# Products with the values in two row tiles of 64 keys, the last 8 keys of all heads in one block, and v loaded over all partitions

## The chip, the core and the metric

The kernel runs on one core of a Trainium2 chip. TensorE (PE; its weight loads are listed as PEld), VectorE (DVE), ScalarE (ACT), GpSimd (POOL) and the DMA queues, of which SyncE (SP) issues most, work side by side and meet at semaphores. The metric is the device time of one execution in microseconds; the time of a kernel is the median of its runs.

## What is computed

An attention over pooled keys and values, then a layer ("mixture of depths") in which only 128 of the 576 rows of each batch go through a dense network. All data is fp32.

```python
B, H, S, D = 8, 8, 576, 64;  pool = 8;  Sp = S // pool          # 72 pooled keys
k_p = k.reshape(B, H, Sp, pool, D).mean(axis=3)
v_p = v.reshape(B, H, Sp, pool, D).mean(axis=3)
scores = scale * np.matmul(q, k_p.transpose(0, 1, 3, 2))
attn = softmax(scores)                                           # over the 72 keys
x = np.matmul(attn, v_p) -> (B, S, H * D)
...
scores = np.einsum('bsd,d->bs', x, w_gate)                       # one gate value per row
for b in range(B):
    top_idx = np.argpartition(-scores[b], capacity)[:capacity]   # the 128 largest
    h = np.maximum(x[b, top_idx] @ w1, 0.0)                      # 512 -> 1024
    out[b, top_idx] += sigmoid(scores[b, top_idx])[:, None] * (h @ w2)
```

## The kernel before

**Order.** `direct_path` first registers about 970 small operations with a planner (`add`: engine, a cost, a function, the buffers that it reads and writes). A list of numbers written out by hand, `ORDER`, then gives the order in which they are issued. Each engine takes its own operations in that order; a number is the position in which the operation was registered. The costs play no part when the kernel runs. Waits follow from the buffers.

**Stages of one batch.** `load_k`, `load_q`, `load_v` are DMAs on SP. `pool_k` and `k_trans` (DVE) add up and transpose the keys into KT; `q_trans` (DVE, L452) transposes q into QT. `scores` (PE, L467) computes the transposed scores, keys on partitions, in 32x32 tiles of the array, 24 matmuls for one parity `s` of the heads and one part `h` of the rows (256 or 320 columns); `CELLS` says which 32 keys of which heads land where. ACT takes the exp into ET (L478). The eight heads' 72 keys make 576 key rows for each of the 8 x 576 query rows, and each parity has four heads, so 288 key rows: three blocks `t`, in which pairs of heads (`PAIRS`) share the 128 partitions, 64 + 64 or 96 + 32 keys at a time.

`pool_v` adds the 8 rows of each value window: on POOL in three steps (L499, L503, L507), in batch 0 and for one block of batch 1 on TensorE with a unit matrix (L494, `sums`), whose result ACT copies out (`copies`, L516). The result is VS, one tile for each block, with two more columns: the constant 8 for the softmax sum, and the product with the gate's weights (`gates`: L522 and the DVE sum L526). `spread` (ACT, L530, seven copies per batch by `PIECES`) then puts the pieces of VS into VP, a tile that is zero elsewhere: each head of a pair has its own columns, so one matmul over 128 keys can serve two heads.

`attend` (L537) forms the product for a chunk of 128 rows (four chunks) or 64 rows (the fifth): for each block and parity one fp32 matmul, ET as the weights, 132 columns of VP moving, accumulated over the three blocks in one PSUM bank for each parity (pA, or pX for some chunks of the first two batches). In the profile an fp32 matmul is two weight loads and two matmuls. `zs` (ACT, L572 and L573) reads the sums and the gate values, `norm` (DVE, L579 and L583) divides, and the rows are stored. `rank` finds the 128 largest rows, a gather brings them back, and `dense` runs them through w1 (`up`, L695) and w2 (`down`, L705) with the whole 128x128 array; its matmuls stand between other batches' work in `ORDER`.

**Opening.** 28 matmuls of zeros (L299) go ahead of the first work of TensorE. ACT fills parts of VR with zeros (L311, four fillings) because some partitions of a block receive no load. `weights` (L339) writes the constant 8 into VS.

**Loads of v.** `RUNS` (L395) has seven DMAs a batch: one of 512 KB and two of 256 KB, over 64 partitions each, and four of 32 KB.

Of the kernel before, what the change touches and what calls it, by code (L numbers as in the profile page):

```python
# [16 lines left out]
def kernel(  # L17
# [34 lines left out]
    54, 53, 1, 35, 56, 0, 4, 2, 38, 57, 5, 37, 32, 6, 33, 36, 34, 51, 7, 8, 39, 9, 10, 50, 52, 11, 12, 40, 62,  # L52
    13, 14, 60, 64, 15, 16, 17, 63, 18, 66, 19, 55, 20, 21, 67, 61, 22, 42, 98, 59, 65, 58, 97, 23, 24, 48, 25,
    46, 78, 26, 49, 77, 27, 68, 44, 28, 45, 81, 29, 43, 30, 47, 31, 41, 106, 96, 70, 74, 88, 71, 105, 85, 72,
    76, 84, 79, 69, 87, 107, 73, 89, 86, 75, 80, 164, 92, 113, 165, 108, 114, 119, 115, 109, 170, 90, 116, 162,
    93, 94, 120, 95, 163, 117, 101, 110, 169, 121, 186, 111, 257, 166, 112, 123, 258, 118, 122, 173, 255, 91,
    193, 256, 103, 124, 174, 104, 83, 187, 102, 252, 180, 194, 179, 195, 99, 254, 125, 196, 188, 126, 189, 100,
    197, 82, 245, 171, 3, 132, 247, 253, 172, 168, 167, 128, 200, 181, 133, 246, 248, 175, 129, 134, 305, 198,
    130, 140, 176, 298, 190, 131, 136, 141, 249, 358, 299, 366, 177, 142, 137, 306, 135, 191, 251, 143, 199,
    250, 201, 192, 138, 127, 178, 300, 307, 285, 362, 313, 182, 202, 144, 203, 145, 204, 360, 286, 146, 206,  # L60
    368, 147, 308, 292, 205, 148, 301, 207, 149, 183, 150, 139, 365, 151, 184, 208, 479, 152, 259, 478, 211,
    153, 185, 154, 361, 287, 155, 209, 156, 288, 309, 210, 215, 157, 312, 291, 158, 359, 212, 310, 367, 289,
    213, 260, 216, 363, 314, 302, 217, 219, 303, 290, 315, 214, 316, 293, 475, 311, 411, 223, 304, 317, 220,
    318, 221, 294, 319, 364, 224, 412, 261, 225, 413, 320, 414, 295, 227, 369, 296, 218, 321, 159, 228, 322,
    229, 371, 297, 263, 370, 324, 264, 372, 471, 418, 373, 472, 265, 325, 230, 326, 419, 262, 270, 222, 415,
    266, 374, 375, 404, 231, 328, 226, 524, 232, 399, 160, 420, 267, 476, 398, 329, 421, 271, 426, 330, 268,
    405, 427, 400, 269, 473, 428, 406, 429, 477, 233, 332, 272, 480, 333, 401, 334, 275, 323, 422, 276, 234,
    402, 235, 482, 336, 481, 403, 430, 483, 273, 236, 277, 484, 274, 485, 407, 337, 237, 417, 432, 238, 431,
    278, 408, 338, 279, 424, 416, 340, 425, 280, 423, 239, 433, 240, 242, 241, 161, 342, 409, 434, 343, 435,
    344, 525, 474, 512, 341, 584, 437, 410, 327, 486, 539, 281, 438, 439, 345, 376, 540, 592, 282, 377, 511,  # L70
    526, 441, 541, 705, 283, 531, 440, 519, 378, 585, 442, 518, 339, 542, 383, 532, 591, 543, 335, 527, 517,
    545, 379, 533, 436, 534, 380, 443, 702, 331, 384, 488, 487, 588, 346, 381, 594, 528, 445, 590, 347, 382,
    587, 597, 593, 513, 348, 703, 349, 388, 514, 350, 385, 446, 351, 389, 595, 386, 637, 447, 390, 387, 535,
    598, 515, 544, 537, 596, 530, 599, 352, 516, 449, 353, 354, 391, 450, 536, 451, 392, 529, 243, 638, 538,
    520, 355, 452, 453, 644, 631, 707, 589, 546, 632, 521, 639, 586, 645, 455, 640, 522, 547, 646, 456, 548,
    457, 647, 448, 630, 393, 817, 523, 652, 698, 489, 697, 550, 490, 601, 458, 600, 454, 648, 491, 444, 551,
    552, 394, 653, 624, 492, 654, 765, 815, 395, 625, 700, 554, 820, 655, 244, 396, 766, 553, 704, 626, 555,
    701, 650, 556, 699, 496, 627, 816, 641, 710, 818, 493, 459, 497, 711, 549, 460, 494, 812, 706, 461, 498,
    814, 495, 462, 628, 649, 463, 558, 750, 629, 642, 464, 633, 559, 560, 465, 501, 468, 656, 743, 658, 502,
    356, 651, 643, 466, 562, 708, 503, 709, 563, 657, 499, 564, 634, 767, 467, 504, 566, 712, 659, 751, 568,  # L80
    635, 660, 752, 569, 661, 567, 500, 570, 810, 469, 738, 561, 663, 636, 768, 662, 284, 769, 737, 505, 664,
    571, 753, 357, 811, 757, 506, 754, 813, 665, 565, 602, 863, 819, 507, 745, 603, 666, 508, 557, 713, 714,
    604, 758, 744, 667, 759, 509, 864, 572, 739, 668, 756, 760, 669, 605, 740, 573, 609, 574, 606, 575, 610,
    470, 576, 607, 577, 741, 608, 761, 857, 671, 578, 672, 614, 742, 579, 673, 580, 611, 755, 763, 850, 615,
    870, 581, 612, 582, 764, 762, 616, 821, 675, 878, 858, 746, 676, 871, 613, 677, 879, 770, 617, 771, 679,
    397, 747, 715, 772, 880, 510, 681, 748, 773, 872, 716, 774, 865, 866, 822, 776, 749, 823, 881, 851, 682,
    618, 683, 873, 777, 678, 680, 867, 717, 856, 775, 619, 874, 778, 718, 684, 670, 824, 620, 674, 719, 621,
    780, 622, 825, 722, 781, 876, 826, 877, 720, 827, 782, 852, 721, 882, 783, 685, 868, 784, 853, 686, 875,
    854, 785, 884, 786, 727, 687, 787, 788, 779, 688, 723, 689, 789, 869, 728, 690, 883, 855, 724, 790, 691,
    859, 694, 792, 692, 693, 885, 860, 794, 793, 729, 795, 886, 796, 887, 725, 623, 861, 583, 726, 797, 889,  # L90
    791, 888, 730, 828, 731, 829, 798, 890, 732, 862, 891, 830, 695, 799, 892, 733, 800, 831, 801, 893, 696,
    832, 894, 895, 734, 833, 735, 897, 802, 834, 835, 898, 899, 840, 803, 836, 901, 804, 902, 837, 807, 805,
    903, 806, 841, 905, 904, 838, 896, 907, 900, 842, 908, 808, 909, 839, 843, 910, 911, 844, 912, 923, 845,
    913, 924, 846, 914, 925, 915, 847, 916, 926, 848, 927, 849, 930, 906, 928, 931, 929, 917, 935, 918, 920,
    919, 968, 967, 932, 936, 933, 937, 934, 969, 921, 938, 970, 736, 809, 945, 939, 946, 940, 947, 941, 948,
    942, 949, 943, 950, 922, 944, 952, 951, 953, 957, 954, 958, 955, 959, 956, 960, 961, 962, 963, 964, 965, 966,
# [55 lines left out]
def direct_path(ctx, tc, q, k, v, moe_w_gate, moe_w1, moe_w2, moe_capacity, out, flag):  # L152
# [3 lines left out]

    nc = tc.nc
# [37 lines left out]
    CELLS = (((0, 1), (0, 2), (0, 0)), ((1, 1), (1, 2), (1, 3)), ((2, 0), (2, 1), (0, 3)), ((2, 2), (2, 3), (1, 0)))  # L195
    PAIRS = ((0, 2), (1, 3), (2, 3))
# [8 lines left out]
    VS = [sb(f"vs{t}", [128, 2, E]) for t in range(NT)]  # L205
    GS = [sb(f"gs{t}", [128, 2, D]) for t in range(NT)]
    VP = sb("vp", [128, 2, NT, 2 * E], n=2)
# [36 lines left out]
    PIECES = (((0, 96, 0), (96, 128, 1)), ((32, 64, 0), (64, 128, 0), (0, 32, 1)), ((0, 64, 0), (64, 128, 1)))  # L244
# [27 lines left out]
    def load(kind, *a, **k):  # L272
        latest[kind] = dma(*a, after=latest.get(kind), **k)
# [15 lines left out]
    def opening():  # L289
# [18 lines left out]
        for i in range(2):  # L308
            for a in (0, 96):

                add("ACT", 1.9, lambda i=i, a=a: nc.scalar.activation(  # L311
                    VR[i][a : a + 32, 0:2].rearrange("p t s d -> p t (s d)"),
                    eps[a : a + 32].rearrange("p (t n) -> p t n", t=1).to_broadcast([32, 2, 2 * POOLW * D]), AF.Copy, scale=0.0),
                    ("eps",), [("VRz", i)], -90 + 10 * i)
        add("PE", 1.1, lambda: nc.tensor.matmul(pM, onerow, wrow, start=True, stop=True), ["onerow", ("SR", 0), ("SR", 1)], ("pM",), -89)  # L315
        for t in range(NT):
            for a, z, m in PIECES[t]:
                def part_of(t=t, a=a, z=z, m=m):
                    nc.scalar.copy(out=WG[a:z, t].rearrange("p s d -> p (s d)"),
                                   in_=pM[a:z, 2 * D * PAIRS[t][m] : 2 * D * (PAIRS[t][m] + 1)])  # L320
                add("ACT", 0.27, part_of, ("pM",), (("WG", t, a),), -60)
# [17 lines left out]
        def weights():  # L339

            for t in (0, 1):
                nc.vector.tensor_scalar(VS[t][:, :, D], places_f[:, 2:3].to_broadcast([128, 2]), 0.0, float(POOLW), op0=OP.is_equal,
                                        op1=OP.mult)
                for a in (32, 64):
                    nc.vector.memset(VS[t][a : a + 32, :, D], float(POOLW))
            nc.vector.memset(VS[2][:, :, D], float(POOLW))
        add("DVE", 0.6, weights, ("places",), [("VS1", t) for t in range(NT)], -85)

    def quiet():
# [6 lines left out]

        add("POOL", 0.79, lambda: nc.gpsimd.memset(VP[0], 0.0), behind, [("VP", 0)], -60, port=True)

        def presets():
            nc.gpsimd.memset(KT[1], 0.0)  # L360
            nc.gpsimd.memset(VP[1], 0.0)
        add("POOL", 1.25, presets, behind, [("KT", 1), ("VP", 1)], -50, port=True)

        def small():
            for x in (*SS, *RZ, RK):
# [790 lines left out]
```

## Time and profile before

| | us |
|---|---|
| median of 3 runs | 255.15 (253.76 to 256.94) |
| the profiled execution | 255.49 |
| its span, first to last instruction | 253.7 |
| PE busy, of the span | 241.7 |
| end of the last matmul in the chain of waits | 246.6 |

A group line of the profile names the source line, the engine, the operation, what it writes and reads, its shape and count, the busy time and the mean ns of one; "128\*64" before a shape means rows and columns of the array that are used. The largest groups that the change touches:

```profile
L557 PEld LDWEIGHTS pA<-vp,et 128*128 128x128 f32 (+1 forms) x420 | 44.8, 179 | 15.3 <-issue 5.9
L557 PE MATMUL pA<-vp,et 128*128 128x132 f32 (+1 forms) x420 | 50.6, 283 | 2.5 <-POOL vr L503 1.4
L530 ACT COPY vp<-vs 32x132 f32<-32x132 f32 (+2 forms) x56 | 16.5, 299 | 6.2 <-DVE vs L526 5.5
```

Matmuls are pipelined, so their durations overlap, and some matmul records are missing: the time that a call of `attend` takes is read from the chain of waits, not from these sums.

### The profile page before, as it was taken

What the parts mean: (1) busy time and instruction counts of PE and PEld (TensorE: products, weight loads), DVE (VectorE), ACT (ScalarE), POOL (GpSimd) and SP (SyncE); (2) the same over time, 40 slices, a digit from 0 to 9 for tenths busy, and PEclk for the clock granted to TensorE, in tenths of its full rate; (3) what the DMA queues carried; (4) which work ended last, traced back from release to release, by engine and by line L of the source; (5) the groups of instructions that cost most, each with busy time, mean ns of one, the idle gap of its engine ahead of it and who ended that gap; (6) DMA issues with size and microseconds to landing.
All of it is one profiled execution on the core that took longest, in us unless ns stands there. A gap on an engine that the chain in (4) does not pass through costs nothing.

```text
span 253.7 us, 7006 instructions
## 1 busy us (share of the span) xinstructions
PE 241.7 (95%) x2844; PEld 172.6 (68%) x2844; DVE 169.6 (67%) x388; ACT 88.9 (35%) x256; POOL 91.8 (36%) x168
## 2 busy tenths in 40 slices
PE   8996899999999999999999999999999999999980
PEld 2594575778865696577857687678776885866830
DVE  4989798979885899767867689586732755420110
ACT  8736364564135312552344123522533023010000
POOL 2258173284800941565028705940040001330101
PEclk9999899999999999999999999999999999999996
DMA  7998999999992799489973951242414104111101
GB/s 252 329 366 301 233 305 369 326 308 262 375 330 77 254 339 290 118 231 302 326 224 106 308 205 41 83 108 90 124 44 152 42 3 146 41 41 47 41 5 48
DMA packets 19338, 48.16 MB, mean 190 GB/s; under 512 B 2249, under 2 KB 2274, under 8 KB 19298
## 3 DMA queue, kind: packets, MB, share of 16 engines
q1 hardware_dynamic: 17986, 43.44, 53.7%
q0 software_dynamic: 1312, 4.20, 5.1%
q8 instruction: 24, 0.39, 0.6%
q14 instruction: 16, 0.13, 0.2%
HBM read 36.08 MB, written 11.55 MB: 188 GB/s over the span
## 4 chain that ended last, share of the span: by engine, by line
PE 94%; DVE 2%; ACT 1%; POOL 1%; issue 0%; POOLq 0%; ACTq 0%
PE pX L695 23%; PE pX L705 23%; PE pA L557 19%; PE pS L467 16%; PE pX L299 4%; PE pA L494 3%; PE pX L557 3%; PE pX L686 1%; PE pM L628 1%; PE pM L652 1%; DVE gs L522 1%; ACT vp L530 0%; PE pM L315 0%; ACT et L478 0%; DVE y L710 0%
## 5 line engine op out<-in xcount | busy, mean ns | idle before, releaser
L695 PEld LDWEIGHTS pX<-xg,w 128*128 128x128 f32 x512 | 62.3, 192 | 13.6 <-issue 13.4
L705 PE MATMUL pX<-w,ht 128*128 128x512 f32 x128 | 64.1, 603 | 0.0
L695 PE MATMUL pX<-xg,w 128*128 128x128 f32 x512 | 64.0, 276 | 0.0
L557 PEld LDWEIGHTS pA<-vp,et 128*128 128x128 f32 (+1 forms) x420 | 44.8, 179 | 15.3 <-issue 5.9
L557 PE MATMUL pA<-vp,et 128*128 128x132 f32 (+1 forms) x420 | 50.6, 283 | 2.5 <-POOL vr L503 1.4
L467 PE MATMUL pS<-qt,kt 32*32 32x256 f32 (+1 forms) x1440 | 45.2, 420 | 0.0
L452 DVE STREAM_TRANSPOSE qt<-qr 128x512 f32<-128x512 f32 (+1 forms) x40 | 38.6, 1006 | 0.0
L499 POOL TENSOR_TENSOR vr<-vr 128x512 f32<-128x512 f32 x20 | 25.7, 1294 | 34.3 <-DMA vr<-in_v_dram 34.3
L640 DVE SCALAR_TENSOR_TENSOR cmp<-sr,sc,lat 128x576 bf16<-128x576 f32 (+1 forms) x40 | 32.5, 812 | 8.3 <-DMA sr<-row 4.5
L478 ACT ACTIVATE et<-pS 128x768 f32<-128x768 f32 (+1 forms) x30 | 26.8, 892 | 25.6 <-PE pS L467 25.6
L467 PEld LDWEIGHTS pS<-qt,kt 32*32 32x32 f32 x1440 | 21.6, 104 | 13.8 <-issue 2.9
L583 DVE TENSOR_TENSOR xs<-pA,rz 128x512 f32<-128x512 f32 (+1 forms) x42 | 25.3, 602 | 6.5 <-DVE rz L579 4.2
L572 ACT ACTIVATE za<-pA,eps 128x8 f32<-128x8 f32 (+1 forms) x42 | 11.1, 264 | 50.2 <-PE pA L557 50.0
L705 PEld LDWEIGHTS pX<-w,ht 128*128 128x128 f32 x128 | 20.6, 191 | 10.6 <-issue 10.1
L660 POOL TENSOR_SCALAR ix<-tk 128x1 int32<-128x1 f32 x8 | 2.0, 249 | 68.9 <-DVE tk L656 55.4
L701 ACT ACTIVATE ht<-pX 128x512 f32<-128x512 f32 x16 | 9.5, 595 | 43.0 <-PE pX L695 43.0
L710 DVE SCALAR_TENSOR_TENSOR y<-pX,gv,xr 128x512 f32<-128x512 f32 x8 | 5.9, 743 | 23.4 <-PE pX L705 21.1
L579 DVE RECIPROCAL rz<-za 128x8 f32<-128x8 f32 (+1 forms) x40 | 7.8, 194 | 20.4 <-ACT za L572 14.8
L714 POOL DMA_INDIRECT out_dram<-y,ix x8 | 8.1, 1010 | 29.9 <-DVE y L710 20.1
L530 ACT COPY vp<-vs 32x132 f32<-32x132 f32 (+2 forms) x56 | 16.5, 299 | 6.2 <-DVE vs L526 5.5
L419 DVE TENSOR_TENSOR kr<-kr 128x640 f32<-128x640 f32 (+1 forms) x16 | 15.7, 993 | 1.5 <-DMA kr<-in_k_dram 1.5
L503 POOL TENSOR_TENSOR vr<-vr 128x256 f32<-128x256 f32 x20 | 15.6, 787 | 0.5
(100 smaller groups left out, 211.2 us busy)
## 6 DMA issues: line engine op xcount, KB each, us to landing
out_dram<-xs SPq DMA_DIRECT2D x32, 256.0 KB
kr<-in_k_dram SPq DMA_DIRECT2D x8, 640.0 KB
qr<-in_q_dram SPq DMA_DIRECT2D x8, 640.0 KB
kr<-in_k_dram SPq DMA_DIRECT2D x8, 512.0 KB
vr<-in_v_dram SPq DMA_DIRECT2D x8, 512.0 KB
qr<-in_q_dram SPq DMA_DIRECT2D x8, 512.0 KB
vr<-in_v_dram SPq DMA_DIRECT2D x16, 256.0 KB
w<-in_moe_w_dram SPq DMA_DIRECT2D x4, 1024.0 KB
```

Of the source, the lines that this page charges most:

```text
L419: e.tensor_tensor(out=x[:, :, 0:2], in0=x[:, :, 0:2], in1=x[:, :, 2:4], op=OP.add)
L452: nc.vector.transpose(out=y.rearrange("p j s (g t) -> p t j s g", t=u), in_=x)
L467: nc.tensor.matmul(banks[t][32 * qd : 32 * qd + 32, 0:n], KT[b % 2][32 * i : 32 * i + 32, j, s, 32 * r : 32 * r + 32], QT[b % 2][h][32 * i ...
L478: add("ACT", 0.2 + 2.4e-3 * n, lambda: nc.scalar.activation(et, pS[:, :, 0:n], AF.Exp, scale=exp_scale), ["pS"], [("ET", b % 2, h, s, t) f ...
L499: e.tensor_tensor(out=x[:, :, 0:4], in0=x[:, :, 0:4], in1=x[:, :, 4:8], op=OP.add)
L503: e.tensor_tensor(out=x[:, :, 0:2], in0=x[:, :, 0:2], in1=x[:, :, 2:4], op=OP.add)
L530: nc.scalar.copy(out=VP[b % 2][a:z, :, t, E * m : E * m + E], in_=VS[t][a:z])
L557: nc.tensor.matmul(acc[s][:, 0 : NP * E].rearrange("p (m d) -> p m d", d=E)[:, p : r + 1 : r - p], ET[i][h][s][:, t, col : col + n], VP[i] ...
L583: nc.vector.tensor_tensor(out=x[:, s], in0=a[:, :, :, 0:D], in1=rz[:, s].to_broadcast([n, s.stop - s.start, NP, D]), op=OP.mult)
L640: nc.vector.scalar_tensor_tensor(cmp[0:n], SR[0:n], SC[i][0:n, c : c + 1], LAT[0:n, LAST - OFF[c] : LAST - OFF[c] + S], op0=OP.subtract, o ...
L695: nc.tensor.matmul(pX[bank][:, cap * f : cap * f + cap], w1[g][:, d, 128 * f : 128 * f + 128], XG[i][:, d, :], start=(d == 0), stop=(d == ...
L705: nc.tensor.matmul(pX[P][0:cap, :], HT[i][f // 4][:, f % 4, :], w2[f // 4][:, f % 4, :], start=(f == 0), stop=(f == FB - 1))
```

## The change

- **Layout.** The 64 first keys of each head lie in blocks 0 and 1, two heads of a parity in the two halves of the partitions; block 2 holds the last 8 keys of all four heads of a parity, 32 partitions for each head (8 of them in use, the rest zero). `CELLS` follows; `PAIRS` is gone.
- **Products.** For blocks 0 and 1 each head has a matmul of its own over its 64 partitions, 66 columns straight from VS; the lower and the upper half of the partitions write to different PSUM banks. Block 2 takes four matmuls for each parity of a 128-row chunk, 64 partitions by 64 rows, 132 columns of VP. A chunk has 16 matmuls instead of 6.
- **VS and VP.** VS has two copies (even and odd batches); only block 2 is spread into VP, in four copies instead of seven. VP shrinks from 792 to 264 columns.
- **Loads.** v comes in four loads of 256 KB over all 128 partitions and four of 32 KB; only block 2 of VR is filled with zeros, one ACT operation for each buffer.
- **Order.** `ORDER` is replaced as a whole. Batch 0 now has `sums` of block 0, two `scores`, the other `sums`, two `scores`, then its five `attend`; before it was three `sums`, three `scores`, and `attend` and `scores` mixed from there.

```diff
 ORDER = (
...
 )
...
-    CELLS = (((0, 1), (0, 2), (0, 0)), ((1, 1), (1, 2), (1, 3)), ((2, 0), (2, 1), (0, 3)), ((2, 2), (2, 3), (1, 0)))
-    PAIRS = ((0, 2), (1, 3), (2, 3))
+    CELLS = (((0, 0), (0, 1), (2, 2)), ((1, 0), (1, 1), (2, 3)), ((0, 2), (0, 3), (2, 0)), ((1, 2), (1, 3), (2, 1)))
...
-    VS = [sb(f"vs{t}", [128, 2, E]) for t in range(NT)]
+    VS = [[sb(f"vs{i}{t}", [128, 2, E]) for t in range(NT)] for i in range(2)]
...
-    VP = sb("vp", [128, 2, NT, 2 * E], n=2)
+    VP = sb("vp", [128, 2, 2, E], n=2)
...
-    PIECES = (((0, 96, 0), (96, 128, 1)), ((32, 64, 0), (64, 128, 0), (0, 32, 1)), ((0, 64, 0), (64, 128, 1)))
+    PIECES = (((0, 64, 0), (64, 128, 2)), ((0, 64, 1), (64, 128, 3)), ((0, 32, 2), (32, 64, 3), (64, 96, 0), (96, 128, 1)))
...
-    RUNS = ((32, 1, 64, 0, 2, 0, 0, 1.62), (0, 1, 64, 2, 1, 2, 0, 1.5), (64, 1, 64, 2, 1, 3, 0, 1.5),
-            (0, 4, 8, 0, 1, 0, 64, 0.23), (96, 4, 8, 0, 1, 2, 64, 0.23), (0, 4, 8, 1, 1, 3, 64, 0.23), (96, 4, 8, 1, 1, 1, 64, 0.23))
+    RUNS = [([[4 * S * D, 2], [POOLW * D, 64], [1, POOLW * D]], 0, 1, t, s, 2 * t + s, 0, 0.8) for t in range(2) for s in range(2)] \
+        + [([[POOLW * D, 8], [S * D, 2], [1, POOLW * D]], 32 * ((i + 2) % 4), 4, 2, 0, 2 * i, 64, 0.23) for i in range(4)]
...
-        for a, z, m in PIECES[t]:
-            def spread(a=a, z=z, m=m):
-                nc.scalar.copy(out=VP[b % 2][a:z, :, t, E * m : E * m + E], in_=VS[t][a:z])
...
+        if t == 2:
+            for a, z, m in PIECES[t]:
+                def spread(a=a, z=z, m=m):
+                    nc.scalar.copy(out=VP[i][a:z, :, m % 2], in_=vs[a:z])
...
         def go():
             for t in range(NT):
-                p, r = PAIRS[t]
+                w = n if t < 2 else n // 2
                 for s in range(2):
-                    nc.tensor.matmul(acc[s][:, 0 : NP * E].rearrange("p (m d) -> p m d", d=E)[:, p : r + 1 : r - p],
-                                     ET[i][h][s][:, t, col : col + n], VP[i][:, s, t, :],
-                                     start=(t == 0), stop=(t == NT - 1), skip_group_check=True)
+                    for u in range(0, n, w):
+                        for a in range(2):
+                            r = 64 * (a if t < 2 else 1 - a)
+                            z = 64 * s + u if split else u
+                            o = banks[a][z : z + w, 0 : NP * E].rearrange("p (m s d) -> p m s d", s=2, d=E)[:, :, s]
+                            o, x = (o[:, t], VS[i][t][r : r + 64, s]) if t < 2 else (o, VP[i][r : r + 64, s])
+                            nc.tensor.matmul(o, ET[i][hf][s][r : r + 64, t, col + u : col + u + w], x,
+                                             start=(t == 0 and (split or s == 0)), stop=(t == NT - 1), skip_group_check=True)
```

`zs` and `norm` read the two banks by halves of the heads instead of by parities; a 64-row chunk in pX takes four readouts of each kind instead of two.

## The prediction

> **What bounds the kernel now.** I read the page first: who is busy, and what the chain that ended last is made of.
>
> ```profile
> PE 241.7 (95%) x2844; PEld 172.6 (68%) x2844; DVE 169.6 (67%) x388; ACT 88.9 (35%) x256; POOL 91.8 (36%) x168
> ...
> PE 94%; DVE 2%; ACT 1%; POOL 1%; issue 0%; POOLq 0%; ACTq 0%
> ```
>
> TensorE carries 94% of the chain; DVE, ACT and POOL hardly enter it. So work taken from those three is worth nothing, and whatever lengthens or shortens TensorE's own sequence moves the end one for one. Next the chain in order of time (start, length, what), in two places:
>
> ```profile
> 72.48 1.29 PE pS L467 x45
> 73.78 0.83 PE pA L557 x12
> 74.60 1.09 PE pX L695 x8
> ...
> 84.18 1.55 PE pA L557 x12
> 85.73 0.86 PE pX L705 x2
> 86.59 0.44 PE pX L686 x4
> 87.02 0.86 PE pX L705 x2
> 87.88 1.35 PE pA L557 x12
> ...
> 97.23 1.06 PE pX L705 x2
> 98.29 0.89 PE pX L695 x8
> 99.18 0.86 PE pX L705 x2
> ```
>
> L557 is the product with the values: six fp32 matmuls, twelve instructions. It takes 1.35 us after another full-array group (87.88) and 1.55 after L467's 32x32 tiles (84.18). L705 takes 0.86 or 1.06, L695 0.89 or 1.09, by the same rule. A change of array form thus costs 0.20 us where 128 weight columns come next. Streaming: 1.35/12 = 0.112 us for 132 columns, 0.86/2 = 0.43 for 512, so 0.84 ns a column, 0.056 us for 66.
>
> Then the instruction durations (min/median/max ns) of one L557 call of 128 rows, one of 64 rows, and of L315, which has a single row of weights:
>
> ```profile
> L557 PE MATMUL pA<-vp,et x12: 276/276/380, 44.4 to 45.7; 128*128 128x132 f32 x12
> ...
> L557 PE MATMUL pA<-vp,et x12: 276/276/327, 103.3 to 103.9; 128*64 128x132 f32 x12
> ...
> L315 PE MATMUL pM<-sr,onerow x2: 587/640/692, 8.3 to 8.8; 1*128 1x512 f32 x2
> ```
>
> The maximum is the first matmul, whose weight load nothing hides: 104 ns for 128 columns, 51 ns for 64, and 105 ns for 128 columns of one single row. So a load costs about 0.81 ns per weight column, however few rows it has. In the steady stream it hides behind the previous matmul (104 against 112). L695 loads 128 columns and streams 128 in 0.89/8 = 0.111, so a load in a stream is 0.104 to 0.111; I take 0.108. This is the row that decides this change. An entry of 0.20 is then a load and some 0.092 of emptying; before 64 columns it is 0.145 (the 64-row call: 0.83 - 6 x 0.112 = 0.16).
>
> **The products, 32 calls of 128 rows.** Now: full array, 12 x 0.112. Changed: blocks 0 and 1 are eight matmuls of 64 keys, weights of 128 columns, 66 moving columns, alternating between two row tiles; four matmuls, so eight instructions, for each tile. Tiles do overlap: L467's twelve cells, in four row groups, do 48 instructions of 256 columns in 1.29 us, where four streams of 0.215 one after the other are already 0.86. But each tile needs eight loads of 0.108 to feed eight streams of 0.056, so the load sets the pace: 0.20 + 7 x 0.108 + 0.056 = 1.01 us. The streaming is halved, the loading is not. Block 2 (last 8 keys of all heads) is four 64x64 tiles with two matmuls each: another form, hence 0.145 + 4 x 0.112 = 0.59. Together 1.60, and always entered from another form.
>
> Before, read against the order list (numbers are those in which the operations are added), 16 calls follow another form and 16 a full-array group: 16 x 1.55 + 16 x 1.35 = 46.4. After: 32 x 1.60 = 51.2. **+4.8 us.** If loads set nothing, a call is 0.20 + 8 x 0.056 + 0.59 = 1.24, in all 39.7, or -6.7: the lower bound. If the two tiles' loads went one after the other, 8 x 0.108 more a call, +27.6: the upper. I stay at 1.60, because L315 prices a load of few rows directly, and in L467 loads in four row groups lengthen the first matmul by 24 ns only (398 against 374), a single 32-column load.
>
> [...]
>
> **Eight calls of 64 rows.** Blocks 0 and 1 are four 64x64 tiles, load 0.05 against stream 0.056: 0.145 + 4 x 0.056 = 0.37. Block 2 is eight 64x32 tiles: 0.092 + 0.025 + 2 x 0.112 = 0.34. Sum 0.71 against 0.83: **-1.0 us** (0 if the tiles start raggedly, as the 0.16 above suggests).
>
> **Who comes next.** Every product now leaves the array in another form than the dense layers use. In the two order lists a full-array operation follows a different form 18 times before, 39 times after: 21 x 0.20 = **+4.2 us**. Bounds: 3 if some of these wait for data anyway, 4.2 if none. The chain shows nothing but TensorE there, so nothing hides it.
>
> **Opening.** Here before loses time:
>
> ```profile
> 22.98 1.80 PE L557 MATMUL pA<-vp,et 128*128 128x132 f32 x12 [1.41 <-POOL vr L503]
> 28.44 1.62 PE L557 MATMUL pA<-vp,et 128*128 128x132 f32 x12 [1.06 <-ACT et L478]
> ...
> 24.00:28.50 4.50, 3.44 (x55) 1.44 (x53) 4.35 (x10) 1.40 (x5) 0.81 (x2) 0.62 0.72 201
> ```
>
> TensorE is idle from about 20.6 to 22.98 (ACT has five copies into VP ahead of the exp that the first product needs); the granted clock then falls (0.62 on average from 24 to 28.5), so that product takes 1.80, not 1.55, and the next scores 2.62, not 1.50; then 1.06 of waiting. Loss 2.4 + 0.25 + 1.1 + 1.0 = 4.8. The new order puts all four scores of batch 0 and its three sums ahead of its products, and only block 2 is copied into VP: four copies of 0.30, not seven of 0.30. Step by step: sums from 11.3, as now (the warm-up matmuls still stand ahead); 1.8; two scores of 1.29; two sums, 3.8; two scores of 1.50; so TensorE has work until about 22.6. The copies, gate and total behind the sums that end at 19.6, and four spreads with an exp between, need some 3 us: 22.7. The product starts without a pause that could drop the clock. **-4.0 us**, of at most 4.8; nothing if a load is late.
>
> Loads: v in four loads of 256 KB over all partitions and four of 32 KB, where three were large. Rates fall to 219-300 GB/s from 8.7 to 12 us, when 64-partition loads of v run, from about 400 before; the new ones may land sooner. One issue more per batch (0.68 us on SP) delays only SP, whose queue is ahead of TensorE outside the opening. VS in two copies frees POOL of 4.7 us of waiting for ACT's copies; 24 copies of 0.30 leave ACT, one of VRz's fillings likewise. None of these is in the chain: nothing, and it costs nothing to lose that cover while TensorE has 94%. The PSUM reads keep their shapes; one 64-row call has four readouts instead of two, some 0.8 us of ACT behind other work.
>
> **Sum.** 4.8 - 1.0 + 4.2 - 4.0 = +4.0 on the span of 253.7: 257.7. Around the span lie 255.49 - 253.7 = 1.8, so 259.5 for this execution. It stands 0.34 above the median of 255.15; I predict **259.5**, +1.7%.
>
> **Rivals.** *Loads hide.* The next load in each tile runs far enough ahead, a call takes 1.24: -6.7 - 1.0 + 4.2 - 4.0 = -7.5, so 247.6. For it: L467's tiles overlap well. [...] *Tiles load one after another (slower):* 259.5 + 27.6 = 287; L467 speaks against it. *Does not do what it says:* if two row tiles did not overlap at all, streams add 8 x 0.056 but loads still pace, near the same 287 or less.
>
> **How the numbers follow.** Two per cent, about what a measurement can tell, is 5.1 us: 250.0 to 260.3. Forecast 72%, by itself 256.5 to 263 (opening 0 to -4.8, entries 3 to 4.2, 64-row calls 0 to -1, load 0.104 to 0.111): a third of that lies above 260.3. Loads hide 14%, nearly all faster. Late loads 9%, slower; serial loads or no overlap 5%, slower. So faster 0.12, within 0.49, slower 0.39. The range leaves out most of the 14% and the 5%: 250.5 to 266.5.
>
> **What would show it.** Matmuls of 66 columns whose starts in one tile are 108 ns apart, not 56; calls of about 1.0 + 0.6 us with a gap between; L695 and L705 at 1.09 and 1.06 more often; no clock dip between 20 and 28 us, and the first product near 22.6. I am wrong if a 128-row call takes under 1.35 us, if the 66-column matmuls come every 56 ns, or if TensorE waits for vr in the opening.

## The result: 379.0 us, and the profile after

The changed kernel takes 379.0 us (median of 4 runs, 377.61 to 385.63), the kernel before on the same chip 256.05 (253.76 to 257.4): a ratio of 1.479, 95% interval 1.465 to 1.492. Medians are over all runs of a kernel; ratios and their intervals leave out runs of over 1.5% above its fastest. The prediction was 259.5 with a range of 250.5 to 266.5. It is wrong by 120 us; of its rivals that of late loads (9%) points at what happened.

The page of the profile after (busy time; granted clock and busy share of the DMA engines in 40 slices, in tenths; the chain of waits by engine and by line):

```profile
PE 274.2 (73%) x3644; PEld 188.6 (50%) x3644; DVE 162.7 (43%) x389; ACT 78.1 (21%) x235; POOL 93.1 (25%) x168
...
PEclk9766995555985899699788958699999999999999
DMA  5444313185149646446634335654412113032100
...
PE 31%; DMA 19%; SPq 10%; issue 4%; DVE 2%; POOL 2%; POOLq 0%; ACT 0%; DVEq 0%
```

The shares are of the whole span, and the chain after can be followed back only to 116 us, so its shares add up to 68%. TensorE had 94% of the span in the chain before; now it has 31%, and DMA and SP's queue, which had no share in it, have 29%. The clock row has half speed in whole slices. Yet the DMA engines are busy for only 0.40 of the span. So the engines wait for transfers, and more than half of the transfer hardware stands idle meanwhile: that pair is what has to be explained. The view of waits names the transfer (us in total, times, longest):

```profile
POOL vr L495 <- DMA vr<-in_v_dram: 102.6, 11, 29.8
...
DVE kr L414 <- DMA kr<-in_k_dram: 57.3, 9, 17.7
...
PE pA L490 <- DMA vr<-in_v_dram: 48.8, 3, 32.7
...
PE pA L559 <- DVE xs L589: 32.3, 9, 8.9
...
DVE xs L589 <- DMA out_dram<-xs: 26.6, 6, 13.1
```

The loads of v come up to 33 us late, and the keys, which stand behind them in SP's queue, up to 18. TensorE itself waits 48.8 us for v, and 32.3 for DVE's normalisation (L589), which waits 26.6 us for stores of the rows; those stand in the same queue. The sign of being wrong that the prediction named, TensorE waiting for vr in the opening, is there. The DMA view of the stretch from 12 to 25 us (40 slices; busy share of the 16 engines in tenths, and what they moved) shows how a load of v runs:

```profile
DMA  9989932211122111111111111110111111111149
GB/s 378 365 334 397 397 145 107 98 66 50 50 82 95 50 50 50 50 50 50 57 50 50 54 63 47 47 63 35 50 50 50 50 50 50 50 50 50 50 126 202
```

At first, with keys and queries, the engines are busy for nine tenths of the time and move 330 to 400 GB/s. Then 50 GB/s at a share of one tenth (0.13 and 51 GB/s from 17 to 22 us, by the windows view), as two engines of sixteen (0.125) would show. At 50 GB/s a 256 KB load takes 5.2 us, and 32 of them 168 us. In the kernel before the same view of the same stretch has a share of 0.9 and 337 GB/s on average.

From TensorE's records I made one account for every kernel below, from 11 us on (about where the first work on zeros ends) to the last matmul: **idle**, gaps of over 0.25 us between one matmul's end and the next one's start; **half clock**, half of the time in which TensorE was busy at a granted clock of 0.5; and the rest, its **own work**.

| profiled execution | idle | half clock | own work |
|---|---|---|---|
| before, 255.49 us | 3.6 | 1.6 | 230.4 |
| after, 380.02 us | 94.1 | 27.8 | 238.2 |
| difference, 124.5 | 90.5 | 26.2 | 7.8 |

The spans differ by 124.4. So 117 of the 124 us are waiting and the half clock that goes with it; the 7.8 us of work are the new products and the dense layers behind them. The windows view (length, busy time and instructions of each engine, clock, DMA share, GB/s) puts a bad stretch beside one in which no more than a single load of v is issued:

```profile
core 0: us, PE busy (x) PEld busy (x) DVE busy (x) ACT busy (x) POOL busy (x), PEclk, DMA share, GB/s
...
60.00:100.00 40.00, 12.34 (x210) 9.10 (x215) 15.55 (x35) 4.54 (x13) 13.51 (x24) 0.59 0.46 148
...
260.00:320.00 60.00, 60.00 (x931) 42.25 (x925) 33.69 (x82) 17.80 (x52) 12.84 (x27) 1.00 0.27 86
```

And in that later stretch the chain (start, length, what) shows the calls of the new product as they are when nothing else is in the way:

```profile
258.75 1.50 PE pS L462 x45
260.26 0.20 PE pM L620
260.46 1.65 PE pA L559 x32
262.11 1.06 PE pX L710 x2
263.17 0.89 PE pX L700 x8
264.06 0.86 PE pX L710 x2
```

A 128-row call takes 1.65 us (1.60 was predicted) and the dense layer behind it 1.06 instead of 0.86, as predicted. In the records of that call the matmuls of 66 columns in one row tile start every 112 ns (108 was predicted, 56 if streaming set the pace), and the other row tile's run 6 ns behind them: the tiles do overlap. The first of block 2's four 64x64 tiles starts 0.20 us after the last matmul of blocks 0 and 1.

### The profile page after: what moved, and what is told of

Its sections match the earlier page's. It is cut to its first block, busy times and chain, and to the rows that moved or that the text cites. A ratio compares the mean times of both kernels' runs of the same rounds, so it can differ in the third digit from the quotient of the medians.

```text
span 378.1 us, 8595 instructions
## 1 busy us (share of the span) xinstructions
PE 274.2 (73%) x3644; PEld 188.6 (50%) x3644; DVE 162.7 (43%) x389; ACT 78.1 (21%) x235; POOL 93.1 (25%) x168
## 4 chain that ended last, share of the span: by engine, by line
PE 31%; DMA 19%; SPq 10%; issue 4%; DVE 2%; POOL 2%; POOLq 0%; ACT 0%; DVEq 0%
DMA vr<-in_v_dram 15%; SPq L279 10%; PE pX L710 10%; PE pX L700 10%; PE pA L559 6%; PE pS L462 3%; DMA out_dram<-xs 2%; DMA xr<-out_dram,ix 2%; POOL vr L495 1%; PE pX L691 1%; DVE qt L447 0%; DVE xs L589 0%; DVE y L715 0%; DVE kh L427 0%; PE pM L657 0%
## 5 line engine op out<-in xcount | busy, mean ns | idle before, releaser
L700 PEld LDWEIGHTS pX<-xg,w 128*128 128x128 f32 x512 | 65.0, 201 | 15.4 <-issue 14.9
L710 PE MATMUL pX<-w,ht 128*128 128x512 f32 x128 | 68.9, 648 | 1.1 <-DMA w<-in_moe_w_dram 1.1
L700 PE MATMUL pX<-xg,w 128*128 128x128 f32 x512 | 67.2, 287 | 2.5 <-DMA w<-in_moe_w_dram 2.5
L559 PE MATMUL pA<-vs,et 64*128 64x66 f32 (+1 forms) x560 | 38.1, 288 | 32.3 <-DVE xs L589 32.3
L559 PEld LDWEIGHTS pA<-vs,et 64*128 64x128 f32 (+1 forms) x560 | 33.0, 195 | 46.4 <-DVE xs L589 32.9
L490 PE MATMUL pA<-vr,ident 128*128 128x128 f32 x64 | 13.6, 404 | 48.8 <-DMA vr<-in_v_dram 48.8
L645 DVE SCALAR_TENSOR_TENSOR cmp<-sr,sc,lat 128x576 bf16<-128x576 f32 (+1 forms) x40 | 33.1, 828 | 19.3 <-DMA sr<-row 14.2
L589 DVE TENSOR_TENSOR xs<-pA,rz 128x512 f32<-128x512 f32 (+1 forms) x42 | 25.3, 602 | 32.3 <-DMA out_dram<-xs 26.6
L490 PEld LDWEIGHTS pA<-vr,ident 128*128 128x128 f32 x64 | 12.9, 310 | 50.2 <-issue 42.5
L414 DVE TENSOR_TENSOR kr<-kr 128x640 f32<-128x640 f32 (+1 forms) x16 | 12.6, 784 | 57.3 <-DMA kr<-in_k_dram 57.3
L462 PEld LDWEIGHTS pS<-qt,kt 32*32 32x32 f32 x1440 | 22.8, 109 | 20.4 <-issue 7.9
L559 PE MATMUL pA<-vp,et 64*64 64x132 f32 (+1 forms) x560 | 24.9, 311 | 0.0
L584 DVE RECIPROCAL rz<-za 128x8 f32<-128x8 f32 (+1 forms) x40 | 7.7, 192 | 36.4 <-ACT za L577 27.7
L719 POOL DMA_INDIRECT out_dram<-y,ix x8 | 8.2, 1024 | 38.1 <-DVE y L715 27.8
L559 PEld LDWEIGHTS pA<-vp,et 64*64 64x64 f32 (+1 forms) x560 | 15.0, 139 | 2.7
```

The source lines that it names most:

```text
L414: e.tensor_tensor(out=x[:, :, 0:2], in0=x[:, :, 0:2], in1=x[:, :, 2:4], op=OP.add)
L462: nc.tensor.matmul(banks[t][32 * qd : 32 * qd + 32, 0:n], KT[b % 2][32 * i : 32 * i + 32, j, s, 32 * r : 32 * r + 32], QT[b % 2][h][32 * i ...
L490: nc.tensor.matmul(o, ident, x[:, :, w], start=(w == 0), stop=(w == POOLW - 1), skip_group_check=True)
L559: nc.tensor.matmul(o, ET[i][hf][s][r : r + 64, t, col + u : col + u + w], x, start=(t == 0 and (split or s == 0)), stop=(t == NT - 1), ski ...
L589: nc.vector.tensor_tensor(out=y[:, a, h], in0=x[:, :, :, 0:D], in1=r.to_broadcast([n, *r.shape[1:3], D]), op=OP.mult)
L645: nc.vector.scalar_tensor_tensor(cmp[0:n], SR[0:n], SC[i][0:n, c : c + 1], LAT[0:n, LAST - OFF[c] : LAST - OFF[c] + S], op0=OP.subtract, o ...
```

## The experiments

The theory after the result: a pattern that leaves a load on two engines. The source pattern of the large loads, `[[4*S*D, 2], [512, 64], [1, 512]]`, has a first count of 2 (two heads), and the share of 0.13 from 17 to 22 us fits two engines of sixteen. That the first count sets the number of engines is a guess at this point; the runs with first counts of 64, 2 and 4 below try it. The rivals: the new order of the operations, the new products, and the mere number of loads on SP. Repeated executions of one kernel spread by 0.4 to 4% here, so each account below belongs to its own profiled execution, whose time is given.

**All large loads with a first count of 64.** The same bytes, cut by halves of the partitions in place of head by head:

```diff
-    RUNS = [([[4 * S * D, 2], [POOLW * D, 64], [1, POOLW * D]], 0, 1, t, s, 2 * t + s, 0, 0.8) for t in range(2) for s in range(2)] \
+    RUNS = [([[POOLW * D, 64], [S * D, 2], [1, POOLW * D]], 64 * a, 1, t, None, 4 * a + 2 * t, 0, 0.8) for t in range(2) for a in range(2)] \
...
-            x = VR[b % 2][:, t, s] if step == 1 else VR[b % 2][row : row + 29 : 4, t]
+            x = VR[b % 2][:, t, s] if step == 1 and s is not None else VR[b % 2][row : row + 64, t] if step == 1 else VR[b % 2][row : row + 29 : 4, t]
```

> The changed kernel with the four large loads of v cut by halves of the partitions (64 partitions, both parities, 256 KB as before) in place of by parity (128 partitions as 2 heads x 64 keys). Nothing else differs. Theory (the load pattern's leading dimension of 2 lets two of the 16 DMA engines carry the load, 50 GB/s in place of about 400): large loads of v run at 220 to 400 GB/s again, no long waits of TensorE for v, and the time falls to what the products and the form changes make, 256 to 263 us. Rival (the new order of the loads on SP and of the batches' work is what waits): stays above 340 us. A 128-row product call stays at 1.6 to 1.65 us in both.

282.07 us (275.45 to 284.13), the kernel before beside it 256.82. So 97 of the 123 us go with the pattern; but it stays about 20 us above the 256 to 263 expected. The edit also changes where a load writes, 64 partitions instead of 128; the run with a first count of 4, below, separates the two.

**Half the dose.** Only the two large loads of block 0 are cut so.

> As the run with all large loads cut by halves, but only block 0's two; block 1's two keep the leading dimension of 2. Theory (two engines carry such a load): 16 loads in place of 32 take about 5.2 us each at 50 GB/s, so 84 us in place of 168, and the time lies about half way, 290 to 330 us. Rival (order of the work): above 340 us.

323.34 us (319.08 to 328.45): a little below the middle between 282 and 379, as a price for each load would have it.

**The same pattern in the kernel before.** Two of its loads, 256 KB each, are cut by parity instead of by partitions; its products and order stay.

```diff
+            dst = x[row : row + step * (rows - 1) + 1 : step, 2 * t : 2 * t + m]
+            if n in (1, 2):
+                s = n - 1
+                src = bass.AP(tensor=v.tensor, offset=v.offset + (H * b + 4 + s) * SP * POOLW * D,
+                              ap=[[2 * S * D, 2], [POOLW * D, 64], [1, POOLW * D]])
+                dst = VR[b % 2][:, 2, s]
```

> The kernel before, with block 2's two large loads of v cut by parity: 128 partitions as 2 heads x 64 keys, the same 256 KB each. Order, products and everything else as before. Theory (two engines): 16 loads of 5.2 us, 84 us of such loads, of which the order of before hides some; 265 to 320 us. Rival (order of the work): 253 to 258 us, as before.

302.67 us, a ratio of 1.184 (1.173 to 1.194), with TensorE's own work no larger, 229.3 us. The pattern alone makes the old kernel 46 us slower. Its DMA view from 24 to 50 us has the same row of fifties:

```profile
DMA  1129699697220007598311199621111121114799
GB/s 54 55 88 143 208 435 351 126 351 301 106 76 25 0 0 87 181 417 342 133 50 25 35 274 284 246 82 50 50 50 50 50 76 50 50 50 82 170 353 271
```

**A first count of 4.** Each large load of after as two of 128 KB, each from one head into 64 partitions (the second DMA is left out here):

```diff
+    RUNS = [([[POOLW * D, 4], [4 * POOLW * D, 16], [1, POOLW * D]], 64 * a, 1, t, None, 4 * a + 2 * t, 0, 0.8) for t in range(2) for a in range(2)] \
...
```

> The changed kernel with each large load of v as two DMAs of 64 partitions and 128 KB from one head, whose source pattern leads with 4 (4 x 16 keys, taken in the order that makes the 4 the outer step, so that keys are paired with other keys' values; only the time is of interest). Theory (the leading dimension is the number of engines): while such a load runs alone, DMA moves about 100 GB/s with a quarter of the engines busy, 84 us of such loads in place of 168; 290 to 335 us. Rival (what is slow is one DMA over 128 partitions from two distant heads): no stretches at 50 or 100 GB/s, about as with halves, 275 to 290 us.

312.2 us (two runs, 310.49 and 313.91), a ratio of 1.227 (1.216 to 1.239). From 12 to 25 us its DMA view begins with a share of two tenths and twice the rate:

```profile
DMA  3222222222224279599997432224439399997339
GB/s 95 95 101 101 107 101 107 101 107 101 110 110 154 101 123 189 189 296 340 284 214 177 101 101 101 95 107 151 145 126 217 126 296 359 416 400 315 151 123 186
```

50 at a count of 2 (in two kernels), 101 at 4 (in one): 25 GB/s for each engine, if the count is the number of engines, which the shares of one and two tenths of sixteen fit. No other small count was run. A load need not write 128 partitions or read two distant heads to be slow: these do neither. That leaves the 25 us between 282 and 256.

**Do the weight loads set the product's pace?** On top of the first experiment, blocks 0 and 1 stream their 66 columns twice, the second time into columns of PSUM that nothing reads.

```diff
+                            if t < 2:
+                                x = VS[i][t][r : r + 64, s : s + 1].to_broadcast([64, 2, E])
+                                o = bass.AP(tensor=o.tensor, offset=o.offset, ap=[o.ap[0], [E if t * s else 4 * E, 2], [1, E]])
```

> As the run with all large loads cut by halves, and in blocks 0 and 1 each product streams its 66 columns twice (132 columns, the second time into unused columns of the PSUM bank). Theory (the weight loads of 0.108 us set the pace there, a stream of 0.056 hides behind them): a 128-row call grows by about 0.05 to 0.1 us, the 64-row call by 0.22, the whole by 3 to 5 us. Rival (streams set the pace): a 128-row call grows by 8 x 0.056 = 0.45 us, the whole by 15 us.

281.96 us (280.74 to 283.28). The whole can't tell the 3 to 5 us expected from none, since the first experiment's runs lie between 275 and 284; the calls can. Chain of the kernel with single streams, then of the one with double streams:

```profile
202.41 1.65 PE pA L559 x32
...
208.23 0.78 PE pA L559 x32
```

```profile
200.71 1.72 PE pA L562 x32
...
206.60 1.00 PE pA L562 x32
```

Twice the columns cost 0.07 us a call where the weights have 128 columns, and 0.22 where they have 64. If streaming set the pace, eight streams of 0.056 would have added 0.45 to the 128-row call. In the records of these calls, the matmuls of one tile behind 128 columns of weights start 112 ns apart with 66 columns to stream and 111 to 116 with 132; behind 64 columns of weights (second and later ones) 58 and 112. So the columns of weights set the pace of the 128-row call. Over all calls the products take 63.0 us instead of 59.0, as 32 x 0.07 + 8 x 0.22 = 4.0 would have it.

**The order.** The new products and the first experiment's loads in the order of before; and the old products and loads in the new order. In both, an operation whose inputs come later in the other order is moved behind them.

> The changed products, layout and copies, with the large loads of v cut by halves of the partitions, but issued in the order of the kernel before: each operation stands where its counterpart stood (block 2 of the change in the place of block 1 of before, block 1 in the place of block 2, two loads of 256 KB in the place of the one of 512 KB; in batch 1 it is block 1 that TensorE adds up). Theory (of the 26 us that are left with good loads, the products and form changes make 9 to 11 and the new order of the loads and of the opening the rest): 263 to 268 us, no half clock after 30 us. Rival (the products and the waits they bring make all of it, whatever the order): 275 to 285 us.

> The kernel before, products, layout and its seven loads of v untouched, issued in the order of the changed kernel (counterparts as in the run with the old order, the other way round; in batch 1 TensorE adds up block 1). Theory (the new order itself loses TensorE time to late loads): 264 to 275 us, with half clock between 25 and 100 us. Rival (the order is as good as the old one): 250 to 257 us.

279.59 (273.24 to 284.44) and 282.75 (276.6 to 285.84). The first lies in the rival's range, the second above both ranges. The account says what of:

| profiled execution | idle | half clock | own work |
|---|---|---|---|
| new order, new products, count 64: 284.13 us | 15.2 | 10.2 | 238.9 |
| the same, double streams: 283.28 | 13.6 | 5.6 | 244.2 |
| old order, new products, count 64: 273.24 | 9.7 | 5.1 | 238.5 |
| new order, old products and loads: 282.54 | 27.7 | 3.6 | 231.3 |

Own work follows the products alone: 229 to 231 us in all runs with the old ones, 238 to 240 with the new, 244 with double streams. What else differs is idling and half clock. What the order is worth these runs do not show: the profile with the new order is the slowest of its four executions, the one with the old order the fastest of its four, and their ranges overlap. The old products and loads in the new order idle most, 27.7 us. In the old order there was something that I can't explain: TensorE stops in the middle of a product, waiting for nothing that the profile shows:

```profile
60.39 1.64 PE pA L561 x31
62.03 3.04 issue
65.08 0.27 PE pA L561
```

A packet of instructions (1.1 us) is under way from 62.3 us while the DMA engines are full (a share of 1.07 from 60 to 66 us). That instructions came late is a guess.

**The opening alone.** The kernel before, with the exp that the first product needs ahead of the copies into VP, and batch 0's four scores ahead of its products.

> The kernel before, only the opening of batch 0 in another order: on ACT the exp of the second scores stands ahead of the six copies into VP that follow, on TensorE all four scores stand ahead of the first product, and the products come in the order 0, 1, 2. Theory (before loses 4.8 us to idling of TensorE from 20.6 to 23 us and the half clock that follows): the first product starts near 23 us with TensorE busy to 22, the clock stays full, 250 to 253 us. Rival (loads set the opening): 254 to 257 us.

256.87 us over 14 runs (254.13 to 263.49), beside 254.27 over 17: a ratio of 1.005 (1.000 to 1.009). No gain: the predicted 4.0 us of the opening are not to be had by this order. Its profile (261.35 us) shows what TensorE meets instead, by the view of waits and, below it, the chain:

```profile
PE pA L560 <- DVE xs L586: 2.8, 1, 2.8
PE pX L470 <- issue: 2.3, 1, 2.3
PE pS L470 <- DVE kt L444: 1.4, 1, 1.4
...
PE pA L497 <- DMA vr<-in_v_dram: 0.7, 2, 0.4
```

```profile
20.40 2.26 issue
...
27.76 0.69 DVE xs L586
28.45 0.19 DVE vs L529
28.65 1.33 DVE kr L422 x2
29.98 1.50 DVE kt L444 x2
31.48 0.56 DVE qt L455
32.04 1.79 DVE ks L426 x2
```

At 20.4 us it stops for 2.3 us in the middle of the scores, again for nothing that the profile shows and again with a packet of instructions under way (1.1 us from 20.2). Then it waits for DVE, which pools and transposes keys and queries ahead of the normalisation. The loads, which the rival named, cost it 0.7 us.

**Where a load writes.** From 12 to 25 us the first experiment's kernel has its DMA engines full and moves 262 GB/s, where the kernel before moves 337: packets of 2 KB took a median of 0.15 us against 0.08. It loads the lower or the upper 64 partitions at a time. So the next kernel loads 128 consecutive rows into all partitions, with a first count of 128:

```diff
+    RUNS = [([[POOLW * D, 128], [1, POOLW * D]], 0, 1, t, s, 2 * t + s, 0, 0.8) for t in range(2) for s in range(2)] \
```

> The kernel after, with each of the four large loads of v taking 128 consecutive rows of v into all 128 partitions (leading count 128 in the source, 256 KB as before; so the upper 64 partitions hold values of other keys and the output is not the reference's). It differs from the repaired loads (282 us, leading count 64, 64 partitions a load) only in where a load writes. In that kernel's opening, packets of 2 KB took a median of 0.15 us from 12 to 25 us, against 0.08 in the kernel before, and 260 GB/s moved against 335. Theory A, a load into 64 partitions is held to about half the rate, however many engines carry it: packets fall back to about 0.08, the queue of the opening empties sooner, and idling plus half clock (25 us from 11 us on) fall by a third to two thirds: 264 to 275 us. Theory B, the packets are slow for another reason (the order of the loads, or the number of loads in flight): 278 to 286.

272.48 us (269.33 to 273.1), within theory A and below every run of the first experiment. The two kernels' DMA views from 12 to 25 us, 64 partitions a load first:

```profile
DMA  9999998999999999989997999998998998999699
GB/s 381 425 413 325 224 236 202 189 192 186 236 230 227 195 164 202 208 239 290 271 287 287 413 359 406 325 271 217 199 154 221 321 252 211 258 277 252 224 271 224
```

```profile
DMA  9999969999999999999998989848977999999988
GB/s 328 403 416 391 347 230 281 381 299 394 425 369 356 425 511 394 394 410 369 350 362 328 372 328 366 347 158 151 202 176 290 347 366 353 359 303 265 277 318 366
```

Full engines with long stretches at some 200 GB/s, then full engines at nearly twice that (262 and 338 on average); the 2 KB packets are back to 0.08 us. Idle and half clock fall from 25.4 in the profile of the first experiment, the slowest of its four executions, to 13.9.

The kernel before shows that it is not the number of partitions alone. Its 512 KB load also writes 64 partitions, but 32 to 95; its two 256 KB loads write 0 to 63 and 64 to 127. By SP's queue the first is what runs from 7.1 to 8.3 us, the other two from 10.4 to 12.3, with busy engines in both stretches:

```profile
DMA packets 237, 0.47 MB, mean 394 GB/s; under 512 B 10, under 2 KB 10, under 8 KB 237
...
DMA packets 262, 0.51 MB, mean 266 GB/s; under 512 B 28, under 2 KB 28, under 8 KB 262
```

Sixty-four partitions across the middle moved 394 GB/s (the next such load, 15.5 to 17.0 us, 381); the two halves' loads, one behind the other in the queue, 266. A busy share of nine tenths therefore doesn't say that the transfers run at their best. Why loads into one half are slower no run here shows.

**Two queues.** Of the first experiment's loads, those into the upper 64 partitions (batches 0 and 1) are issued by ACT; and the same for one load of the kernel before.

```diff
+                 cost=0.66, eng="ACT" if b < 2 and step == 1 and row == 64 else "SP")
```

> The kernel with the repaired loads (282 us), with the loads into the upper 64 partitions of batches 0 and 1 issued by ScalarE, so that they stand in another queue than those into the lower 64. Theory A (a load into 64 partitions goes at half rate by itself, two into different halves go at full rate together): 268 to 279 us. Theory B (rate is shared anyway): 280 to 286; on ScalarE the two loads of batch 0 go out ahead of all else, and may delay the keys, so a few us more are possible under both.

> The kernel before, with the 256 KB load of v into partitions 64 to 127 of batches 0 and 1 issued by ScalarE instead of SP, beside the one into partitions 0 to 63. Theory A (half rate for 64 partitions alone): the first product finds its values up to 1.3 us earlier, and the dip of the clock after it may go (1.6 us): 251 to 254.5 us. Theory B: 254 to 257, no difference.

278.95 us (276.38 to 281.96), 3 less than the 282.07 of one queue, with the ranges overlapping: inconclusive, though it moved 311 GB/s in that stretch instead of 262. The kernel before became slower: 258.93, a ratio of 1.013 (1.008 to 1.018), outside both theories. Its idling is 7.5 us instead of 3.6, and begins with waits of the sums for v at 10.8 and 14.0 us. Two queues gave less here than one load over all partitions.

**All partitions and the old order.**

> The new products in the order of before, with each large load of v as 128 consecutive rows into all partitions (values of other keys, as in the run that loaded all partitions). TensorE's own work beside waits was 238.5 to 239.1 us from 11 us on in the runs with the new products, 230.4 in the kernel before. If what is left of the loss is waiting in the opening, set by how fast v arrives, then idling and half clock come down from 15 us (old order, 64 partitions a load) to 5 to 10: 262 to 269 us. If the old order is spoilt by its mended dependencies, as its stalls in the middle of a product suggest, it stays at 270 to 280. A time at or under 258 would say that the products cost nothing.

272.77 us (268.73 to 274.53), above the 262 to 269 and in the 270 to 280 of the other theory. The profiled execution was the shortest of the four, 268.73, and its account is within what was expected: 3.8 idle, 5.9 half clock, 239.1 work, without a stall inside a product. So with good loads both orders have a median of 272 to 273. No kernel that was run is faster than the one before.

## Why the prediction was wrong, step by step

**The step that failed is the price of the loads.** "Loads: v in four loads of 256 KB over all partitions ... the new ones may land sooner", costed at nothing. That takes a load's time from its bytes and from the rates of the loads before. What was not read is the line of the diff that stands ahead of the prediction: the pattern changes its first count from 64 to 2. No row of the trace before could show it, since the loads of v there have first counts of 64 and 8. Measured: 50 GB/s, so 168 us for the 32 loads, and 90.5 us of idling and 26.2 of half clock more than before. By the accounts, idling and half clock come to 121.9 us with the count of 2, 25.4 with 64 and half of the partitions, 13.9 with 128 and all partitions, and 5.2 in the kernel before.

That loads over all partitions may land sooner was sound in itself (338 GB/s against 262). But the rates that the prediction put down to loads over 64 partitions belong, by the rows above, to loads into one half; the large load into 32 to 95 was not slow.

**The rival of late loads** (9%, slower) had the right direction: TensorE idles (94.1 us in the profile after), and the clock falls (27.8 us of half clock). But its time was to lie within a range that ends at 266.5. The loads were slow of themselves (50 GB/s), and the keys and the stores came to wait behind them.

**The products, +4.8 - 1.0.** Right in mechanism. A call is 1.65, not 1.60, and 0.78, not 0.71 for 64 rows: 32 x 1.65 + 8 x 0.78 = 59.0, against 46.4 + 8 x 0.83 = 53.0 before, so +6.0 for +3.8. From the records of the products' matmuls, each counted from the end of the one before, half clock taken out, it is 54.0 before, 58.4 after and 59.2 with loads over all partitions: +4.4 to +5.2. The 64-row call's 1.0 of gain was 0.4. The rival in which loads hide (1.24 a call) falls with the 1.65 and the double streams.

**Who comes next, +4.2.** Right. Counted in the same way, the two dense layers and their transposes take 118.9 us of TensorE in the kernel before and 122.9 after: +4.0.

So the sum for TensorE, +8.0, was 7.8 in the profile after and 8.1 to 9.6 in those of the same products with other loads. With loads of a first count of 128 over all partitions the whole is 272.5 us, and its profiled execution 17.4 above that of before: 8.7 are own work (239.1 - 230.4), and 8.7 idling and half clock (13.9 - 5.2).

**The opening, -4.0.** Wrong, and it would have been wrong with good loads too. It was read as a matter of order, because the chain there has ACT's copies and an exp in it. The order alone gained nothing in the kernel before. DVE is busy there for 26.9 of the 30 us from 10 to 40 us, and the DMA engines are at a share of 0.96; what is moved forward in the order met DVE's work next, and a stop that stays unexplained. With loads over all partitions the changed kernel does pass 20 to 28 us without a pause, as predicted, and then idles 0.9 us at 30.8 and 2.5 at 33.1 (ahead of the sums of batch 1, behind DVE's normalisation), with 3.4 us of half clock after it. So the loss moved by some 10 us and kept its size (5.1 us, against 4.7 before).

**The chances.** The forecast's 72% rested on TensorE's own work, which came out to within 2 us, and on an opening that waits for no load, which it does. What was missing is a case "a load is much slower than its bytes", and the range had no such end.

What stays open: the stops for nothing that the profile shows (3.0 us inside a product, 2.3 inside scores), and how much of the last 8.7 us another order could win back; no order was made for the new loads.

## What to carry to other kernels

When a change touches a DMA's access pattern, price the load by its first count and by the partitions that it writes before its bytes: here 256 KB cost 5.2 us at a first count of 2, and in stretches with busy engines, loads into the lower or the upper 64 partitions moved 262 to 266 GB/s, loads across both halves 338 to 394 (means of stretches in which other loads run too). Waiting engines together with a low DMA share (0.40 of the span, 0.13 while such a load ran) pointed at the pattern, not at bandwidth; a full share at a lower rate (262 GB/s from 12 to 25 us, against 338 with loads over all partitions) pointed at where the load writes. Splitting this fp32 product into smaller matmuls saved nothing where the weight loads set the pace (112 ns from start to start, 1.65 us a call against 1.35 to 1.55), and cost each full-array neighbour 0.2 us (1.06 against 0.86).

## What the hardware showed that was not expected

- At small first counts the rate of a load followed the count: 50 GB/s at 2 and 101 at 4.
- Issues on SP grew long behind such loads: up to 7.6 us for a small load of v and 4.6 for a large one (1.4 at most in the kernel before), and what stood behind them in the queue came later still. In the view of SP's issues for v (count; ns min/median/max), the kernel after:

```profile
L279 SPq DMA_DIRECT2D vr<-in_v_dram x64: 541/703/7604, 1.2 to 271.2; - x64
```

- Idling cost twice. In the kernel before, idling of 0.6 us at 20.5 and of 1.4 us at 21.6 is followed by 3.4 us at a granted clock of 0.5 from 24.2. In the kernel after, the pieces at 0.5 last 3.4, 6.8, 10.2 or 13.7 us, and once 37.5 (from 55.5); 1.9 us of idling at 199.5 is followed by 3.4 us from 202.3. In the kernel with all partitions, 2.3 us of idling at 145.7 is followed by 6.8 us from 149.0. Not each pause did it: 2.95 us at 255.2 in the kernel after was followed by none.
- Sixty-four partitions are not alike: 394 GB/s into 32 to 95, 266 into 0 to 63 and 64 to 127, in the same kernel.
